# Making the second layer's weight from all partitions, in a fused FFT, soft-MoE and squared-ReLU kernel

## The chip, the core and the metric

The kernel runs on one core of a Trainium2 chip. Its engines are called by the profile's names: PE (matrix multiply; PEld is its weight load), DVE (vector), ACT (activations and copies), POOL (general), SP (issues most DMAs). The metric is the device time of one execution in microseconds, as the median of several runs; less is better.

## The reference

The input x is 8 x 3072 x 256. The reference takes the real part of a two-dimensional FFT, then a soft mixture of experts over tokens, then a feed-forward layer with a squared ReLU:

```python
x = fft(fft(x, axis=1), axis=2).real.reshape(24576, 256)
logits = x @ phi                                # 32 slots, 4 for each of 8 experts
slot_in = softmax(logits, axis=0).T @ x         # 32 x 256
slot_out[e] = relu(slot_in[e] @ w1[e]) @ w2[e]  # w1: 256 x 1024, w2: 1024 x 256
x = softmax(logits, axis=1) @ slot_out
h = x @ w_in                                    # 256 x 2048
out = (s * relu(h)**2 + b) @ w_out              # 2048 x 256
```

## The kernel before, in words

The last two products are turned round: h = c @ G, where c are the 32 softmax coefficients of a token and G = slot_out @ w_in is a 32 x 2048 matrix. Both are held as float16 pairs of a high and a low part, so that a token has 128 numbers, and G (tile g16) has 128 partitions: its high part twice, then its low part twice.

The part that the change touches begins near 199 us of the span. The experts' slots go through w1 (`e_up`, L899) and are turned on PE (`e_turn`, L919). Then `e_down` (L931 to L948) multiplies by w2: experts 0 to 3 are group eg=0, experts 4 to 7 eg=1, and each of a group's four experts sits in its own 32 columns of the PE array (`tile_position=(0, 32 * cg)`). The loop runs over 8 slices f of the hidden features, with the expert cg as the inner loop; half 0 is f = 0 to 3, half 1 is f = 4 to 7. w2 comes through SP's queue (L801 to L814): experts 0 to 3 whole, then the first halves of 4 to 7, then quarters. A float32 product shows as two PE records.

Before `e_down`, the coefficients of chunk 0 are copied on DVE (`c_two`, L779) and turned by two DMA transposes (`c_turn`, L784). After it, PE picks each expert's slots with a selection matrix (L987), ACT copies them out (sot), the largest absolute value is brought to all partitions through two transposes and a product (L1009 to L1023), and one product with four 32-column tiles makes G (L1015). ACT and DVE round it to gs; its first 512 features are copied into g16 by ACT and DVE, the other 1536 by 12 DMAs of 32 partitions each (L1032 to L1034).

The main stage (L1052 to L1142) makes 64 blocks of 384 tokens. For a block, `emit_h(n, p)` makes 256 of the 2048 features of block n: two products into the PSUM tile fhp (pool ps_f, two buffers), ReLU and scale on ACT to r (L1062), max times r on DVE to r2 (L1063). At its end it calls `finish()` (L1039), which takes the previous emission's r2, casts it to float16 (L1048, high part a) and subtracts (L1049, low part l). In block n of `finish`, the cast is ACT's and the subtraction DVE's, but for n < 2 the emissions with p % 4 = 2 have their cast on DVE, and those with p % 4 other than 0 their subtraction on POOL. So the ACT queue holds, in this order, r of an emission and then the cast of the one before it. The order of each queue is the order of the program: the kernel has a manual schedule.

`dots(op, n, t, f)` (L1081) is the work of a unit: one product of 512 columns with the high part and one of 256 columns with the low part, for one of three groups t of 128 tokens and one of 16 feature slices f. A block has 48 units. Blocks 1 to 63 finish one t before the next; between their units the emissions for the following block stand, one for every 6 units. Block 0 goes feature by feature: all three t for each f, so that it can begin once the first emissions are there. Three emissions stand ahead of it, and 13 among its 48 units: its own other five and all eight of block 1. `result` (L1089) scales and adds the bias: on DVE alone in blocks 0 and 63, and by ACT, POOL and DVE in the others.

## Time and profile before

| what | value |
| --- | --- |
| median of 3 runs | 1402.54 us (1401.94 to 1404.03) |
| the profiled execution | 1404.25 us, of which the span is 1402.5 us |
| mean granted TensorE clock | 0.998 |
| DMA, mean over the span | 80 GB/s |

The span is the time from the first to the last instruction of the core. A row of the profile names the line of the kernel, the engine, the operation and its tiles (out<-in); a number behind "idle before" or in brackets is the time the engine stood still just before, with what ended it. The timeline gives the start of a group of like instructions, the time from its first start to its last end, and their count. The windows give, for a stretch, the busy time of each engine and the granted clock.

### The profile page before, as it was taken

What the parts mean: (1) busy time and instruction counts of PE and PEld (TensorE: products, weight loads), DVE (VectorE), ACT (ScalarE), POOL (GpSimd) and SP (SyncE); (2) the same over time, 40 slices, a digit from 0 to 9 for tenths busy, and PEclk for the clock granted to TensorE, in tenths of its full rate; (3) what the DMA queues carried; (4) which work ended last, traced back from release to release, by engine and by line L of the source; (5) the groups of instructions that cost most, each with busy time, mean ns of one, the idle gap of its engine ahead of it and who ended that gap; (6) DMA issues with size and microseconds to landing.
All of it is one profiled execution on the core that took longest, in us unless ns stands there. A gap on an engine that the chain in (4) does not pass through costs nothing.

```text
span 1402.5 us, 23190 instructions
## 1 busy us (share of the span) xinstructions
PE 1379.1 (98%) x9026; PEld 844.8 (60%) x9026; DVE 1151.8 (82%) x1485; ACT 1002.3 (71%) x1407; POOL 316.6 (23%) x290
## 2 busy tenths in 40 slices
PE   9989998999999999999999999999999999999998
PEld 6667554566666666666666666666666666666665
DVE  1567745998989898989898989898888888888885
ACT  2676115787777777778787777777877777777773
POOL 1145202422222121212121212122212121112110
PEclk9999999999999999999999999999999999999999
DMA  8997993101010101011110101010101010101000
GB/s 348 414 318 296 380 410 106 36 24 36 24 33 23 36 21 36 23 32 28 27 30 24 36 24 33 24 36 21 35 23 37 23 37 20 37 23 37 23 20 27
DMA packets 74526, 112.89 MB, mean 80 GB/s; under 512 B 35792, under 2 KB 61264, under 8 KB 67120
## 3 DMA queue, kind: packets, MB, share of 16 engines
q1 hardware_dynamic: 74288, 111.31, 24.0%
q8 instruction: 71, 1.16, 0.4%
q14 instruction: 39, 0.32, 0.1%
q0 software_dynamic: 128, 0.10, 0.0%
HBM read 78.48 MB, written 25.17 MB: 74 GB/s over the span
## 4 chain that ended last, share of the span: by engine, by line
PE 88%; DVE 2%; DMA 1%; ACT 1%; issue 0%; SPq 0%; POOL 0%; ACTq 0%; POOLq 0%; DVEq 0%
PE op L1085 46%; PE op L1087 23%; PE fhp L1058 11%; PE racc L725 3%; DMA w2t<-in_moe_w_dram 1%; PE hp L650 1%; PE dps L710 1%; DVE r L1063 1%; DVE rhl L1049 0%; SPq L1034 0%; PE lp L189 0%; PE lp L567 0%; PE ehp L905 0%; ACT r L1062 0%; DVE cm L582 0%
## 5 line engine op out<-in xcount | busy, mean ns | idle before, releaser
L1085 PE MATMUL op<-whl,rhl 128*128 128x512 f16 x3072 | 1025.9, 379 | 0.0
L1087 PE MATMUL op<-whl,rhl 128*128 128x256 f16 x3072 | 837.4, 273 | 0.3 <-DVE rhl L1049 0.3
L1062 ACT ACTIVATE r<-fhp,wsc 128x768 f32<-128x768 f32 x512 | 458.9, 898 | 157.4 <-PE fhp L1058 154.6
L1063 DVE SCALAR_TENSOR_TENSOR r<-fhp,r 128x768 f32<-128x768 f32 x512 | 484.2, 949 | 25.1 <-ACT r L1062 23.2
L1085 PEld LDWEIGHTS <-rhl 128*128 128x128 f16 x3072 | 300.6, 98 | 335.3
L1049 DVE TENSOR_TENSOR rhl<-r,rhl 128x768 f16<-128x768 f32 x500 | 489.6, 981 | 3.3 <-ACT rhl L1048 0.9
L1048 ACT CAST rhl<-r 128x768 f16<-128x768 f32 x508 | 419.4, 826 | 75.6 <-DVE r L1063 75.3
L1095 POOL TENSOR_TENSOR o<-o,bias 128x256 f32<-128x256 f32 x186 | 203.4, 1094 | 881.2 <-ACT o L1094 876.4
L1087 PEld LDWEIGHTS <-rhl 128*128 128x128 f16 x3072 | 300.6, 98 | 62.5 <-DVE rhl L1049 0.7
L1058 PE MATMUL fhp<-ct,g 128*128 128x384 f16 x1024 | 249.9, 326 | 3.9 <-DVE r L1063 2.9
L1097 DVE SCALAR_TENSOR_TENSOR ot<-op,small,o 128x256 f32<-128x256 f32 x192 | 92.7, 483 | 104.6 <-POOL o L1095 104.3
L1058 PEld LDWEIGHTS <-g 128*128 128x128 f16 x1024 | 100.0, 98 | 71.6 <-issue 4.1
L1094 ACT ACTIVATE o<-op,small 128x256 f32<-128x256 f32 x186 | 88.2, 474 | 17.5 <-PE op L1087 17.4
L393 PE MATMUL vt<-xb,phd 128*64 128x512 f32 (+3 forms) x288 | 47.9, 467 | 5.3 <-DMA xb<-in_x_turned_dram 5.3
L725 PE MATMUL racc<-xrt,dh 128*64 128x256 f32 x384 | 44.5, 383 | 0.4 <-DVE dh L715 0.4
L393 PEld LDWEIGHTS vt<-xb,phd 128*64 128x64 f32 x288 | 25.0, 136 | 26.3 <-issue 8.6
L725 PEld LDWEIGHTS racc<-xrt,dh 128*64 128x64 f32 x384 | 26.3, 137 | 20.9 <-issue 4.9
L418 DVE COPY v<-vq 128x512 f32<-128x512 f32 (+1 forms) x15 | 8.3, 593 | 34.8 <-PE vq L414 34.8
L405 ACT COPY vts<-vt 128x512 f32<-128x512 f32 (+1 forms) x16 | 8.5, 532 | 35.8 <-PE vt L393 35.7
L463 ACT COPY tt<-tps 32x512 f32<-32x512 f32 x48 | 27.7, 576 | 5.3 <-PE tps L449 4.8
L1049 POOL TENSOR_TENSOR rhl<-r,rhl 128x768 f16<-128x768 f32 x12 | 20.1, 1686 | 39.6 <-DMA g<-gs 33.0
L772 POOL TENSOR_TENSOR lg<-lg,rm 112x512 f32<-112x512 f32 x16 | 22.5, 1407 | 4.2 <-DVE rm L770 4.2
...
## 6 DMA issues: line engine op xcount, KB each, us to landing
xb<-in_x_turned_dram SPq DMA_DIRECT2D x24, 1024.0 KB, 20.1
...
out_dram<-ot SPq DMA_DIRECT2D x128, 128.0 KB, 1.7
...
out_dram<-ot SPq DMA_DIRECT2D x128, 64.0 KB, 2.0
...
```

The source lines that it names most:

```text
L393: nc.tensor.matmul(vt[64 * h:64 * h + 64, o:o + k, :], lhsT=phd[:, c, sg, :], rhs=turned(pg, c, i, k, rev), start=(c == 0 and m < 2), stop ...
L725: nc.tensor.matmul(raccs[acc][64 * h:64 * h + 64, :], lhsT=dh[:, m, g].rearrange("p j e -> p (j e)"), rhs=xr[k][0][:, g, t, :], start=(sum ...
L1048: (nc.vector.tensor_copy if n < 2 and p % 4 == 2 else nc.scalar.copy)(a, r2)
L1049: (nc.gpsimd if far else nc.vector).tensor_tensor(out=l, in0=r2, in1=a, op=ALU.subtract)
L1058: nc.tensor.matmul(hp[:, k, :].rearrange("p (s b m) -> p s b m", s=2, b=B), lhsT=g16[:, f * P:(f + 1) * P], rhs=c, start=True, stop=True)
L1062: nc.scalar.activation(out=r, in_=hp, func=AF.Relu, scale=wsc[:, 2, p:p + 1])
L1063: nc.vector.scalar_tensor_tensor(out=r2, in0=hp, scalar=0.0, in1=r, op0=ALU.max, op1=ALU.mult)
L1085: nc.tensor.matmul(op.rearrange("p h d -> p (h d)"), lhsT=a, rhs=w.rearrange("p h d -> p (h d)"), start=(f == 0), stop=False)
L1087: nc.tensor.matmul(op[:, 0, :], lhsT=l, rhs=w[:, 0, :], start=False, stop=(f == NFC - 1))
L1094: nc.scalar.activation(out=o1, in_=op[:, 1, :], func=AF.Copy, scale=qv)
L1095: nc.gpsimd.tensor_tensor(out=o1, in0=o1, in1=bias, op=ALU.add)
L1097: nc.vector.scalar_tensor_tensor(out=ot, in0=op[:, 0, :], scalar=qv, in1=o1, op0=ALU.mult, op1=ALU.add)
```

## The change

* w2: experts 4, 5 and 6 come in two halves each, expert 7 as a half, a quarter and two eighths. In `e_down(1, 1)` the loops are exchanged: the expert cg is the outer loop, the feature slice f the inner.
* Coefficients of chunk 0: no DMA transposes and no copies for them; PE turns them with 32 products (`ct_turn`) between the two groups of `e_down`, and ACT and DVE copy them out.
* Slots: the selection matrix is repeated four times, so that sot has the 32 slots four times in its 128 columns (`e_slots`); the first group's part is done before the second group's `e_down`. The maxima go through a product with the selection matrix (`e_tops`) in place of two transposes and a product.
* G: features 0 to 1023 are made in four products on all 128 rows (`g_dot`), rounded straight into g16 by ACT, and on the low rows by DVE (`g_out`). Features 1024 to 2047 go as before, by 16 DMAs (`g_rest`). Two of the four products, and `g_rest`, stand behind the first two emissions.
* Blocks 0 and 1 both go feature by feature. Two emissions stand ahead of them, and 22 among their 96 units, the first at unit 3 and the last at unit 91, 4.2 units apart on average: the rest of block 0, block 1, and block 2. `finish()` is called ahead of each of these emissions, too. The first unit's products are split in two, so that those with the high part can go first. The sharing of casts and subtractions with DVE and POOL holds for n < 3.
* The warming products (keep_warm) of this part are gone.

The diff, cut to its core:

```diff
-        c = (slice(0, 4), slice(4, 6), slice(0, 8), slice(6, 8))[h]
-        dma_ready(2.57 * (0.5, 0.25, 1, 0.25)[h])
+        c = (slice(0, 4), slice(4, 6), slice(0, 8), slice(4, 8), slice(6, 7), slice(7, 8))[h]
...
-    todo += [(h == 0, lambda e=e, h=h: w2_load(e, h)) for h in (0, 1, 3) for e in range(4, 8)]
+    parts2 = [(e, 0) for e in range(4, 8)] + [(4, 3), (5, 3), (6, 3), (7, 1), (7, 4), (7, 5)]
+    todo += [(h == 0, lambda e=e, h=h: w2_load(e, h)) for e, h in parts2]
...
-    sot = late.tile([P, 2, NE], F32, name="sot")
+    sot = ctp.tile([P, 2, P], F32, name="sot")
...
+    sel4 = ep.tile([P, 2, 4, NE], F32, name="sel4")
+    nc.gpsimd.tensor_copy(sel4, sel_sb.unsqueeze(2).to_broadcast([P, 2, 4, NE]))
+    selm = ep.tile([P, 2, NE], F32, name="selm")
+    id16 = ep.tile([P, P], F16, name="id16")
+    nc.gpsimd.tensor_copy(id16, ident)
...
-        for f in range(4 * half, 4 * half + 4):
-            for cg in range(4):
-                nc.tensor.matmul(
-                    op[32 * cg:32 * cg + 32, :], lhsT=hTs[eg][:, f, 32 * cg:32 * cg + 32],
-                    rhs=w2t[4 * eg + cg][:, f, :],
-                    start=(f == 0), stop=(f == FF1 // P - 1), tile_position=(0, 32 * cg), skip_group_check=True,
-                )
+        fs, cgs = range(4 * half, 4 * half + 4), range(4)
+        for f, cg in [(f, cg) for cg in cgs for f in fs] if eg and half else [(f, cg) for f in fs for cg in cgs]:
...
-        (nc.scalar.copy if eg else nc.vector.tensor_copy)(so[:, eg, :], op)
-        nc.vector.tensor_reduce(out=small[:, 18 + eg:19 + eg], in_=op, axis=AX.X, op=ALU.max, apply_absolute_value=True)
+        if eg:
+            for c in range(2):
+                nc.scalar.copy(so[:, eg, c * P:(c + 1) * P], op[:, c * P:(c + 1) * P])
+        else:
+            nc.vector.tensor_copy(so[:, eg, :], op)
+        top = small[:, 18 + eg:19 + eg]
+        nc.vector.tensor_reduce(out=top, in_=op, axis=AX.X, op=ALU.max, apply_absolute_value=True)
+        nc.vector.tensor_scalar(out=selm[:, eg, :], in0=sel_sb[:, eg, :], scalar1=top, scalar2=None, op0=ALU.mult)
...
+    spt, top4 = [], []
+
+    def e_slots(eg):
+
+        if eg == 0:
+            spt.extend(pse.tile([P, P], F32, tag="sp", name="sp_", bufs=2) for _ in range(2))
+        for c in range(2):
+            nc.tensor.matmul(spt[c], lhsT=so[:, eg, c * P:(c + 1) * P], rhs=sel4[:, eg].rearrange("p r n -> p (r n)"),
+                             start=(eg == 0), stop=(eg == 1))
+
+    def e_tops(eg):
+
+        if eg == 0:
+            top4.append(pse.tile([P, P], F32, tag="tps", name="top4", bufs=1)[:, 0:NE])
+        nc.tensor.matmul(top4[0], lhsT=ones, rhs=selm[:, eg, :], start=(eg == 0), stop=(eg == 1))
...
+        tp = pse.tile([P, 8, P], F16, tag="eh", name="ctt", bufs=3)
+        a = lgc(0).rearrange("p k g e -> p (k g e)").bitcast(F16).rearrange("p (h k m) -> p h k m", h=2, k=8)[:, h]
+        for k in range(8):
+            for q in (0, 64):
+                nc.tensor.transpose(tp[q:q + 64, k, 0:R], a[:, k], id16[:R, :R], tile_position=(0, q))
+        (nc.vector.tensor_copy if h else nc.scalar.copy)(cts[0][:, h], tp[:, :, 0:R])
+
+    e_down(0, 0)
+    e_down(0, 1)
     for h in range(2):
-        c_two(0, h, ep)
-        c_turn(0, h)
-    warm = pse.tile([P, P], F32, tag="mx", name="warm")
-    for eg in range(2):
-        for h in range(2):
-            keep_warm(warm, (0,0,0,0)[2 * eg + h])
-            if eg == 1 and h == 0:
-                while side_step(0.0, True):
-                    pass
-                mxp[:] = [pse, 1]
-                for f in wim_steps[:-1]:
-                    f()
-            e_down(eg, h)
-    for f in wim_steps[-1:]:
+        ct_turn(h)
+    e_slots(0)
+    while side_step(0.0, True):
+        pass
+    mxp[:] = [pse, 1]
+    for f in wim_steps[:-1]:
         f()
+    e_down(1, 0)
+    wim_steps[-1]()
+    nc.vector.tensor_scalar(out=wim, in0=wim, scalar1=D / GMAX, scalar2=None, op0=ALU.mult)
+    e_tops(0)
+    e_down(1, 1)
     drop(hTk[0])
-    keep_warm(warm, 2)
-    sp_ = pse.tile([P, 2, NE], F32, tag="sp", name="sp_")
+    e_slots(1)
+    e_tops(1)
     for c in range(2):
-        for eg in range(2):
-            nc.tensor.matmul(sp_[:, c, :], lhsT=so[:, eg, c * P:(c + 1) * P], rhs=sel_sb[:, eg, :],
-                             start=(eg == 0), stop=(eg == 1))
-    nc.scalar.copy(sot, sp_)
-    keep_warm(warm, 0)
+        nc.scalar.copy(sot[:, c, :], spt[c])
+    qv, ga, gsc = [small[:, k:k + 1] for k in range(15, 18)]
+    nc.vector.tensor_reduce(out=ga, in_=top4[0], axis=AX.X, op=ALU.max)
+    nc.vector.tensor_scalar(out=ga, in0=ga, scalar1=wim, scalar2=1e-15 * D / GMAX, op0=ALU.mult, op1=ALU.max)
+    nc.vector.reciprocal(gsc, ga)
...
-        mt = psf.tile([P, 2, 512], F32, tag="fhp", name="mt")
-        row = small[0:1, 13:14]
-        nc.tensor.transpose(mt[0:1, 0, 0:P], small[:, 18:19], ident)
-        nc.tensor.transpose(mt[0:1, 0, P:2 * P], small[:, 19:20], ident)
-        nc.vector.tensor_reduce(out=row, in_=mt[0:1, 0, 0:2 * P], axis=AX.X, op=ALU.max)
-        gp = pso.tile([P, 512], F32, tag="op", name="gp")
-        for c in range(2):
+        gps = {}
+        HC = 2 * P
+
+        def g_dot(j):
+
+            gps[j] = pso.tile([P, 512], F32, tag="op", name="gp")[:, 0:HC]
+            for c in range(2):
+                nc.tensor.matmul(gps[j], lhsT=sot[:, c, :], rhs=wi[c][:, HC * j:HC * j + HC], start=(c == 0), stop=(c == 1))
+
+        def g_out(j):
+
+            g, gp = g16[:, HC * j:HC * j + HC], gps.pop(j)
+            nc.scalar.activation(out=g, in_=gp, func=AF.Copy, scale=gsc)
+            nc.vector.scalar_tensor_tensor(out=g[64:P], in0=gp[64:P], scalar=gsc[64:P], in1=g[64:P], op0=ALU.mult, op1=ALU.subtract)
+
+        def g_rest():
+
+            gp = pso.tile([P, 512], F32, tag="op", name="gr")[:, 0:HC]
+            for c in range(2):
+                for j in range(4):
+                    nc.tensor.matmul(
+                        gp[32 * j:32 * j + 32, :], lhsT=sot[:, c, 0:NE], rhs=wi[c][:, HC * (4 + j):HC * (5 + j)],
+                        start=(c == 0), stop=(c == 1), tile_position=(0, 32 * j), skip_group_check=True,
+                    )
+            gs = frp.tile([P, 2, HC], F16, tag="r", name="gs")
+            nc.scalar.activation(out=gs[:, 0], in_=gp, func=AF.Copy, scale=gsc)
+            nc.vector.scalar_tensor_tensor(out=gs[:, 1], in0=gp, scalar=gsc, in1=gs[:, 0], op0=ALU.mult, op1=ALU.subtract)
             for j in range(4):
-                nc.tensor.matmul(
-                    gp[32 * j:32 * j + 32, :], lhsT=sot[:, c, :], rhs=wi[c][:, 512 * j:512 * j + 512],
-                    start=(c == 0), stop=(c == 1), tile_position=(0, 32 * j), skip_group_check=True,
-                )
-            if c == 0:
-                nc.tensor.matmul(mt[:, 1, 0:1], lhsT=ones[0:1, :], rhs=row, start=True, stop=True)
-                nc.vector.tensor_scalar(out=ga, in0=mt[:, 1, 0:1], scalar1=wim, scalar2=1e-15 * D / GMAX,
-                                        op0=ALU.mult, op1=ALU.max)
-                nc.vector.reciprocal(gsc, ga)
-        warm = pso.tile([P, 512], F32, tag="op", name="warm")[:, 0:P]
-        keep_warm(warm, 6)
-        gs = frp.tile([P, 2, 512], F16, tag="r", name="gs")
-        nc.scalar.activation(out=gs[:, 0], in_=gp, func=AF.Copy, scale=gsc)
-        nc.vector.scalar_tensor_tensor(out=gs[:, 1], in0=gp, scalar=gsc, in1=gs[:, 0], op0=ALU.mult, op1=ALU.subtract)
-        for r in range(4):
-            eng = nc.vector.tensor_copy if r // 2 else nc.scalar.copy
-            eng(g16[32 * r:32 * r + 32, 0:512], gs[0:32, r // 2])
-        for j in range(1, 4):
-            for r in range(4):
-                nc.sync.dma_start(out=g16[32 * r:32 * r + 32, 512 * j:512 * j + 512], in_=gs[32 * j:32 * j + 32, r // 2])
+                for r in range(4):
+                    nc.sync.dma_start(out=g16[32 * r:32 * r + 32, HC * (4 + j):HC * (5 + j)], in_=gs[32 * j:32 * j + 32, r // 2])
+
+        for j in range(2):
+            g_dot(j)
+        for j in range(2):
+            g_out(j)
...
-                far = n < 2 and p % 4
-                (nc.vector.tensor_copy if n < 2 and p % 4 == 2 else nc.scalar.copy)(a, r2)
+                far = n < 3 and p % 4
+                (nc.vector.tensor_copy if n < 3 and p % 4 == 2 else nc.scalar.copy)(a, r2)
...
-        def dots(op, n, t, f):
+        def dots(op, n, t, f, part=2):
...
-            nc.tensor.matmul(op.rearrange("p h d -> p (h d)"), lhsT=a, rhs=w.rearrange("p h d -> p (h d)"),
-                             start=(f == 0), stop=False)
-            nc.tensor.matmul(op[:, 0, :], lhsT=l, rhs=w[:, 0, :], start=False, stop=(f == NFC - 1))
+            if part != 1:
+                nc.tensor.matmul(op.rearrange("p h d -> p (h d)"), lhsT=a, rhs=w.rearrange("p h d -> p (h d)"),
+                                 start=(f == 0), stop=False)
+            if part:
+                nc.tensor.matmul(op[:, 0, :], lhsT=l, rhs=w[:, 0, :], start=False, stop=(f == NFC - 1))
...
-        for p in range(3):
+        for p in range(2):
             emit_h(0, p)
-            keep_warm(warm, (0,4,0)[p])
-        ops = [pso.tile([P, 2, D], F32, tag="op", name="op") for _ in range(3)]
-        units = [(f, t) for f in range(NFC - 2) for t in range(3)]
+        g_dot(2)
+        g_out(2)
+        g_rest()
+        g_dot(3)
+        g_out(3)
+        finish()
+        units = [(f, t) for t in range(3) for f in range(2)] + [(f, t) for f in range(2, NFC - 2) for t in range(3)]
         units += [(f, t) for t in range(3) for f in (NFC - 2, NFC - 1)]
-        at = [k * 48 // (16 - 3) for k in range(16 - 3)]
-        for u, (f, t) in enumerate(units):
-            while at and at[0] <= u:
-                at.pop(0)
-                emit_h(*divmod(16 - len(at) - 1, 8))
-            dots(ops[t], 0, t, f)
-            if u == 27:
-                nc.vector.tensor_tensor(out=qv, in0=ga, in1=ga, op=ALU.mult)
-                nc.vector.tensor_tensor(out=qv, in0=qv, in1=wa, op=ALU.mult)
-                nc.vector.tensor_tensor(out=qv, in0=qv, in1=sb_in[:, 0:1], op=ALU.mult)
-                for k in wik:
-                    drop(k)
-            if f == NFC - 1:
-                result(ops[t], 0, t)
-        for k in rhk.pop(0):
-            drop(k)
-        for n in range(1, NBLK):
+        first = [(0, t) for t in range(3)] + [(1, t) for t in range(3)] + units[6:]
+        emits = {3 + k * 21 // 5: divmod(k + 2, 8) for k in range(22)}
+        for n, order in enumerate((first, units)):
+            ops = {}
+            for u, (f, t) in enumerate(order):
+                if 48 * n + u in emits:
+                    finish()
+                    emit_h(*emits.pop(48 * n + u))
+                if f == 0:
+                    ops[t] = pso.tile([P, 2, D], F32, tag="op", name="op")
+                if n == 0 and f == 0:
+                    dots(ops[t], n, t, f, 0)
+                else:
+                    dots(ops[t], n, t, f)
+                if n == 0 and (f, t) == (0, 2):
+                    for k in range(3):
+                        dots(ops[k], n, k, f, 1)
+                if n == 0 and u == 27:
+                    nc.vector.tensor_tensor(out=qv, in0=ga, in1=ga, op=ALU.mult)
+                    nc.vector.tensor_tensor(out=qv, in0=qv, in1=wa, op=ALU.mult)
+                    nc.vector.tensor_tensor(out=qv, in0=qv, in1=sb_in[:, 0:1], op=ALU.mult)
+                    for k in wik:
+                        drop(k)
+                if n and u in (8, 20):
+                    c_two(1, u // 20, frp)
+                if n and u in (14, 26):
+                    c_turn(1, u // 26)
+                if f == NFC - 1:
+                    result(ops[t], n, t)
...
+        for n in range(2, NBLK):
```

## Rows read from the trace of the kernel before

**Rows 1.** The page's first part: busy time, share of the span, instructions.

```profile
PE 1379.1 (98%) x9026; PEld 844.8 (60%) x9026; DVE 1151.8 (82%) x1485; ACT 1002.3 (71%) x1407; POOL 316.6 (23%) x290
```

**Rows 2.** Windows of blocks 0, 1 and 2: length, busy us, clock, DMA share, GB/s.

```profile
231.39:253.75 22.36, 20.63 (x122) 11.54 (x120) 19.60 (x24) 18.64 (x24) 16.23 (x10) 1.00 0.03 9
253.75:272.78 19.03, 18.52 (x112) 10.94 (x112) 17.41 (x26) 13.95 (x18) 5.89 (x5) 1.00 0.24 58
272.78:290.98 18.20, 18.20 (x114) 10.96 (x112) 16.86 (x23) 14.50 (x21) 6.96 (x6) 1.00 0.06 20
```

**Rows 3.** Waits of PE, 225 to 265 us: total, times, longest.

```profile
PE fhp L1058 <- DVE r L1063: 2.9, 7, 0.8
```

**Rows 4.** Timeline, PE and DVE, 183 to 213 us.

```profile
183.23 1.02 PE L710 MATMUL dps<-ht__1653,ft_sb 128*128 128x512 f32 x2
184.19 3.67 PE L725 MATMUL racc<-xrt,dh 128*64 128x256 f32 x32
...
209.14 4.35 PE L937 MATMUL eop<-w2t,hT 128*32 128x256 f32 x70
...
212.87 0.42 DVE L944 COPY so<-eop 128x256 f32<-128x256 f32 x1 [1.91 <-PE eop L937]
```

**Rows 5.** The tile of w2: durations in ns (least, median, most), first and last start.

```profile
L937 PE MATMUL eop<-w2t,hT x128: 379/379/403, 209.1 to 220.3; 128*32 128x256 f32 x128
```

**Rows 6.** Timeline of PE's weight loads, the last wait for w2.

```profile
219.59 0.57 PEld L937 LDWEIGHTS eop<-w2t,hT 128*32 128x32 f32 x10 [0.58 <-DMA w2t<-in_moe_w_dram]
```

**Rows 7.** Timeline from w2's end to the first emission, 220 to 228 us.

```profile
220.68 0.37 ACT L944 COPY so<-eop 128x256 f32<-128x256 f32 x1 [12.84 <-PE eop L937]
...
221.08 0.42 DVE L945 TENSOR_REDUCE small<-eop 128x1 f32<-128x256 f32 x1 [7.45 <-ACT so L944]
...
226.21 7.92 SPq L1034 DMA_DIRECT2D g<-gs  x12
...
227.74 0.81 PE L1058 MATMUL fhp<-ct,g 128*128 128x384 f16 x4 [0.82 <-DVE g L1031]
```

**Rows 8.** Timeline of ACT and DVE at the first emissions, 228 to 231 us.

```profile
228.26 1.69 ACT L1062 ACTIVATE r<-fhp,wsc 128x768 f32<-128x768 f32 x2 [0.80 <-PE fhp L1058]
...
229.19 1.82 DVE L1063 SCALAR_TENSOR_TENSOR r<-fhp,r 128x768 f32<-128x768 f32 x2 [1.60 <-ACT r L1062]
...
230.18 0.83 ACT L1048 CAST rhl<-r 128x768 f16<-128x768 f32 x1 [0.23 <-DVE r L1063]
...
230.92 0.89 ACT L1062 ACTIVATE r<-fhp,wsc 128x768 f32<-128x768 f32 x1
```

**Rows 9.** Timeline of DVE, PE and ACT, 248 to 260 us.

```profile
248.13 0.55 DVE L1048 CAST rhl<-r 128x768 f16<-128x768 f32 x1
248.60 0.95 DVE L1063 SCALAR_TENSOR_TENSOR r<-fhp,r 128x768 f32<-128x768 f32 x1
...
256.02 0.49 PE L1058 MATMUL fhp<-ct,g 128*128 128x384 f16 x2
...
258.66 0.83 ACT L1048 CAST rhl<-r 128x768 f16<-128x768 f32 x1 [2.32 <-DVE r L1063]
259.40 1.69 ACT L1062 ACTIVATE r<-fhp,wsc 128x768 f32<-128x768 f32 x2
```

**Rows 10.** The page's costliest groups: busy us, mean ns, idle before.

```profile
L1095 POOL TENSOR_TENSOR o<-o,bias 128x256 f32<-128x256 f32 x186 | 203.4, 1094 | 881.2 <-ACT o L1094 876.4
...
L1097 DVE SCALAR_TENSOR_TENSOR ot<-op,small,o 128x256 f32<-128x256 f32 x192 | 92.7, 483 | 104.6 <-POOL o L1095 104.3
...
L1094 ACT ACTIVATE o<-op,small 128x256 f32<-128x256 f32 x186 | 88.2, 474 | 17.5 <-PE op L1087 17.4
...
L1049 POOL TENSOR_TENSOR rhl<-r,rhl 128x768 f16<-128x768 f32 x12 | 20.1, 1686 | 39.6 <-DMA g<-gs 33.0
```

**Rows 11.** Windows, as rows 2, of two stretches with little PE work.

```profile
104.00:108.00 4.00, 2.26 (x24) 1.68 (x18) 3.97 (x8) 1.19 (x4) 0.00 (x0) 0.75 1.00 416
228.00:232.00 4.00, 2.62 (x17) 1.60 (x14) 2.77 (x4) 3.51 (x5) 0.00 (x0) 1.00 0.20 53
```

More of the change, by code (lines that the diff above doesn't have):

```diff
@@ L611, in tile_fft2__then__softmoe__then__act_relu2 @@
     tpool.release()
-    late = tc.alloc_tile_pool(name="late", bufs=1)
     hpool = tc.alloc_tile_pool(name="hpool", bufs=1)
@@ new lines, in ct_turn @@
+    def ct_turn(h):
+        if h == 0:
+            cts[0] = ctp.tile([P, 2, B, R], F16, name="ct", bufs=1)
+        tp = pse.tile([P, 8, P], F16, tag="eh", name="ctt", bufs=3)
[4 more added lines that the diff above has]
+        (nc.vector.tensor_copy if h else nc.scalar.copy)(cts[0][:, h], tp[:, :, 0:R])
@@ L991, in tile_fft2__then__softmoe__then__act_relu2 @@
+    nc.vector.reciprocal(gsc, ga)
     pse.release()
     ep.release()
-    qv, ga, gsc = [small[:, k:k + 1] for k in range(15, 18)]
-    nc.vector.tensor_scalar(out=wim, in0=wim, scalar1=D / GMAX, scalar2=None, op0=ALU.mult)
     for _ in range(2):
@@ new lines, in tile_fft2__then__softmoe__then__act_relu2 @@
+        for n, order in enumerate((first, units)):
[25 more added lines that the diff above has]
+                    result(ops[t], n, t)
+            for k in rhk.pop(n):
+                drop(k)
@@ L1143, in tile_fft2__then__softmoe__then__act_relu2 @@
     ctp.release()
-    late.release()
     pools[1][0].release()
```

6 lines of the change are left out of this document (added).

## The prediction

> **What bounds the kernel now.** Read the totals first: PE is busy for 98% of the span [rows 1], so only PE's work and its gaps count. The windows then say where the gaps are. Block 2 is dense: 18.20 us for 48 units and 8 emissions [rows 2]. A unit streams 512 + 256 columns and an emission 2 x 384, so each takes 18.20/56 = 0.325 us. From the first unit at 231.39 us to the start of block 2 at 272.78 us 41.4 us pass [rows 2], and 96 units and the 20 emissions in between need 116 x 0.325 = 37.7 us. So blocks 0 and 1 hold 3.7 us of gaps, and PE's waits name what ends most of them: the DVE's r2 (L1063), which frees the buffer that an emission writes [rows 3]. All after 272.78 us is the same work before and after the change. What the change can give or cost is therefore read from one number: how long after w2's last product block 2 starts. That product starts at 220.3 us [rows 5], so now it is 52.5 us. I call its start E now and E' after.
>
> **Part a, E' itself: +3.0 us.** Now the last wait for w2 ends at 219.59 us [rows 6]: the transfers set E. Afterwards PE has more to do ahead. The first 64 records of w2 begin at 209.14 us, and the last starts 0.38 us before the copy at 212.87 us, so at 212.5 us: 0.053 us a record [rows 4, 5]. Behind them come 32 small products that turn the coefficients. No row shows them; bounds are half of that step, 0.9 us, and the 0.106 us of a record in 64 columns ((3.67 - 0.38)/31 [rows 4]), 3.4 us. I take the narrow tiles' 0.053, 1.7 us: they are the nearest. Then four passes of 128 columns for the slots, each half of the 0.213 us worked out below: 0.4. The first half of the second group takes 32 x 0.053 = 1.7, and w_in's maximum, its copy and the product for the first tops, one behind the other, 0.9: no row has them at these sizes; they lie between nothing and three steps of 0.38 us [rows 5, 7]. That is 217.2 us.
>
> Now the exchanged loop. Two float32 passes of 512 columns end 1.02 us after the first start [rows 4]: twice the streaming of 512 columns and one drain. One pass of 256 columns lasts 0.38 us [rows 5]: its streaming and one drain. The difference is three times the streaming of 256 columns, which is 0.213 us. The 0.106 us in 64-column tiles and the 0.053 us in 32-column tiles are that number divided by two and by four: neighbouring records run side by side because they lie in different tiles. With the expert outside, eight records in a row lie in one tile, and nothing runs beside them. An expert then holds PE for 7 x 0.213 + 0.05 us until the next begins: 3 x 1.54 + 1.49 = 6.1 us in all, where 32 x 0.053 = 1.7 would do. E' = 223.3, which is +3.0. Bounds: if the passes overlapped after all, the transfers would set the end, now with two records in place of ten behind the last piece, -0.7; with slow turns +3.9. The smaller pieces of expert 7 therefore gain nothing: PE comes to them late. The removed DMA transposes lay behind w2 in SP's queue, and I cost that at nothing.
>
> **Part b, from E' to the first emission: -3.5 us.** Now 227.74 - 220.3 = 7.4 us [rows 5, 7]. After: 0.38 for the product; two half copies on ACT, between 0.37 (one whole) and 0.74, taken 0.5; the DVE's maximum 0.42, which again follows ACT's copy [rows 7]; the product with the selection about 0.2 on DVE (between 0 and 0.48, a DVE operation on 256 columns [rows 10]); the two passes for the tops 0.4. Four 256-column passes for G go beside three small DVE operations and end at 2.9 us; ACT's rounding takes 0.47 and DVE's 0.48 [rows 10]: 3.9 us. The added copies on POOL (the repeated selection, the float16 identity) lie ahead of the turns, beside `e_up` and w2's first group, where POOL has no work; without that cover they would cost some 1.1 us each, as a POOL operation on 256 columns does [rows 10].
>
> **Part c, the emissions: the step that decides.** `finish()` is now called ahead of each emission among the units, so ACT's queue holds the cast of the previous emission in front of the next r. The cast waits for r2, r2 for r. Rows of the first emissions give this chain: r starts at 228.26, r2 ends at 230.14, the cast starts at 230.18, and the next instruction of ACT at 230.92 [rows 8]. So from one r to the next 2.66 us must pass, where the program gives 4.2 units and an emission, 1.69 us. Block 1 has one such place already (the `finish()` at unit 5): the products for the next r were issued at 256.02, but ACT stood at the cast until 258.66 and took up r at 259.40 [rows 9].
>
> One emission in four has its cast on DVE. There the next r is not held (0.85 us a piece [rows 8]); its r2 starts behind r2 and cast on DVE, 1.92 + 0.47 us after the r before [rows 8, 9], ends 0.95 later, and with 0.03 and 0.74 the r after that stands 4.11 us behind. Four emissions take 2.66 + 2.66 + 4.11 = 9.4 us, 2.36 each. PE cannot run ahead of it, since fhp has two buffers: an emission waits for the r2 of the one two before it.
>
> The first emission among the units needs G's third part. Second emission at E' + 4.8; cast of the first 4.4 + 1.92 to 7.15; DVE's subtraction to 8.2; rounding on DVE 0.48: E' + 8.6. From there to block 2's first emission are 22 steps, 22 x 2.36 = 51.9: E' + 60.5, against 52.5 now. Parts b and c together: +8.0 us. The first half of G in the pause, the split first units and the 16 small transfers (0.66 us each, 7.92/12 [rows 7], about 10.6 us from E' + 8) lie under this chain. Bounds +6.5 (head 0.8 shorter, first gaps shared) to +10 (DVE subtractions slowed beside POOL).
>
> **Part d, block 2: +1.5 us.** Block 1 now ends for all three t within its last five units. Three bias additions of 1.09 us on POOL, behind subtractions of 1.69 us for block 2, hold DVE's last step of each result, and so the next r2 [rows 10]. Between 0, if the gaps of part c leave POOL ahead, and 3. I take the middle.
>
> **Sum.** +3.0 + 8.0 + 1.5 = +12.5 us on the profiled execution (span 1402.5, its own time 1404.25, 1.7 above the median). The median becomes 1402.54 + 12.5 = 1415.0 us. About 0.2%, 2.8 us, can be told from no change.
>
> **Rivals.** First, *faster*: the cast ahead of r costs nothing because something holds PE's emissions further apart than the chain needs, or ACT reaches the cast with r2 done. It decides at a distance of 2.36 us between emissions. Then 118 pieces of 0.325 us follow the first unit at E' + 7.7: block 2 at E' + 46.1, -6.4 us, with part a -3.4: 1399.1 us. The gaps of rows 3 speak against it; for it only that the program places them 1.69 us apart. Chance 0.10.
>
> Second, *no change*: the same, but today's 3.7 us of gaps stay: +0.3, 1402.8 us. Chance 0.06.
>
> Third, *the clock*: with 28% gaps PE falls to half clock, 1.2 GHz. In a stretch with PE busy for 2.26 of 4 us the mean granted clock was 0.75, so half of it at the lower level; with 2.62 of 4 us it stayed at 1.00 [rows 11]. An emission's share of 1.69 us would take 3.38, 22 x (3.38 - 2.36) = 22 us more: 1437 us. The Trainium skill (TensorE: Matmul & The Clock Gate, section "A second HAM failure mode: psum-queue depth-cycling") says that frequent short idling between groups of matmuls can make the clock swing between its levels. The second of rows 11, the nearer to the forecast's 72%, speaks against it. Chance 0.03.
>
> That the exchanged loop does what it is for (last piece, two records) is the lower bound of part a: 1411.3, inside the forecast.
>
> **How the numbers follow.** The forecast has 0.81: its bounds are -0.7 + 6.5 + 0 = +5.8 and +3.9 + 10 + 3 = +16.9, so 1408 to 1420, and I give 1407 to 1420. Outside lie the three rivals with 0.19. Faster 0.10, same 0.06, slower 0.84.
>
> **What will show it.** ACT's casts (L1048) preceded by waits for r2, some 16 times; PE's waits for L1063 near 15 us in blocks 0 and 1; emissions 2.4 us apart; w2's last product near 223 us with no wait for w2 before it; first emission some 4 us later. If emissions come 1.7 us apart, part c is wrong and with it the sign.

## The result and the profile after

The changed kernel takes 1415.72 us (median of 5 runs, 1414.81 to 1416.79) against 1402.54 us: a ratio of 1.0091, 95% interval 1.0076 to 1.0105. It is slower by 13.2 us. Its profiled execution took 1415.72 us with a span of 1414.0 us.

First the page of the changed kernel: busy time and share, then two groups of instructions (busy us, mean ns, idle before and what ended it).

```profile
PE 1380.4 (98%) x9050; PEld 846.4 (60%) x9050; DVE 1148.7 (81%) x1484; ACT 1002.0 (71%) x1410; POOL 325.2 (23%) x298
...
L1090 ACT CAST rhl<-r 128x768 f16<-128x768 f32 x506 | 417.6, 825 | 92.5 <-DVE r L1105 92.4
...
L1100 PE MATMUL fhp<-ct,g 128*128 128x384 f16 x1024 | 250.1, 326 | 12.0 <-DVE r L1105 11.2
```

PE does 1.3 us more work than before [rows 1]. Most of the rest is waiting: 11.2 us of it ahead of the emissions, for DVE's r2 (2.9 us before [rows 3]). The line numbers have moved: r is now L1104, r2 L1105, the cast L1090, the emission's products L1100.

To compare stretches I count from the experts' first upward product, which is untouched: 198.85 us before, 196.03 us after. The front part before it differs by 2.8 us between the two profiled executions although nothing in it was changed: over the profiled executions of this document this product starts between 193.85 us (e8) and 200.03 us (e10). The timeline of PE from there:

```profile
207.43 3.64 PE L942 MATMUL eop<-w2t,hT 128*32 128x256 f32 x58 [0.47 <-DMA w2t<-in_moe_w_dram]
211.00 0.98 PE L1001 MATMUL ctt<-id,lg 112*64 112x112 f16 x32
...
212.55 1.93 PE L942 MATMUL eop<-w2t,hT 128*32 128x256 f32 x32
...
215.38 4.59 PE L942 MATMUL eop<-w2t,hT 128*32 128x256 f32 x32
...
222.02 1.97 PE L1049 MATMUL gp<-wi,sot 128*128 128x256 f32 x8 [0.38 <-DVE small L1025]
224.26 0.50 PE L1100 MATMUL fhp<-ct,g 128*128 128x384 f16 x2 [0.28 <-DVE g L1055]
```

The exchanged loop is the one of 4.59 us, the loop with the feature outside the one of 1.93 us above it. Three cuts through the records of the exchanged loop (the tile of w2 with durations in ns, then first and last start) show how it runs:

```profile
L942 PE MATMUL eop<-w2t,hT x4: 379/379/403, 215.4 to 216.1; 128*32 128x256 f32 x4
...
L942 PE MATMUL eop<-w2t,hT x6: 379/379/379, 217.4 to 217.8; 128*32 128x256 f32 x6
...
L942 PE MATMUL eop<-w2t,hT x4: 379/379/379, 219.0 to 219.6; 128*32 128x256 f32 x4
```

The first four and the last four records start 0.216 us apart (0.24 us the first time); the 24 between come in pairs, one pair for every 0.216 us. Four records, one for each expert, last 0.40 us in place of 0.38 us and wait for a piece of w2; they start at 215.38, 216.28, 217.17 and 218.06 us. I read this so: the records of one expert, which lie in one tile, do not overlap, but PE takes up the next expert beside the fifth of the eight records of the one before. An expert then holds the next back by 0.89 us, and the mean over the loop is (4.59 - 0.38)/31 = 0.136 us a record, against (1.93 - 0.38)/31 = 0.050 us with the feature outside.

The last record starts at 219.60 us, 23.56 us after the first upward product (21.41 before, where it starts at 220.26 us). The first emission follows 4.67 us later (7.48 before).

The windows of blocks 0, 1 and 2 (length, busy time of PE, PEld, DVE, ACT, POOL, clock, DMA share, GB/s), to be set against [rows 2]:

```profile
228.34:254.29 25.95, 20.81 (x121) 11.54 (x120) 17.19 (x23) 14.55 (x20) 12.49 (x8) 1.00 0.04 11
254.29:282.20 27.91, 20.43 (x118) 11.14 (x116) 16.99 (x25) 17.14 (x23) 13.79 (x9) 1.00 0.13 31
282.20:302.44 20.24, 18.52 (x113) 10.94 (x113) 16.58 (x24) 14.84 (x23) 11.63 (x10) 1.00 0.10 30
```

Blocks 0 and 1 hold 5.1 and 7.5 us of gaps (length less PE's busy time; 1.7 and 0.5 before). PE is busy for 80% and 73% of them, and no other engine for more than 66%: none is full. Block 2 begins 86.17 us after the first upward product (73.93 before) and block 3 106.41 us after it (92.13 before): 14.3 us more. A block begins here with the first emission that stands among its units (it makes features of the next block). What fills the gaps is a chain between engines. Waits of PE, 212 to 300 us:

```profile
PE fhp L1100 <- DVE r L1105: 11.2, 14, 1.5
PE op L1128 <- DVE ot L1141: 1.8, 1, 1.8
```

And the timeline of ACT in block 1:

```profile
256.77 0.83 ACT L1090 CAST rhl<-r 128x768 f16<-128x768 f32 x1 [1.02 <-DVE r L1105]
257.50 0.90 ACT L1104 ACTIVATE r<-fhp,wsc 128x768 f32<-128x768 f32 x1
260.32 0.83 ACT L1090 CAST rhl<-r 128x768 f16<-128x768 f32 x1 [1.92 <-DVE r L1105]
261.06 1.69 ACT L1104 ACTIVATE r<-fhp,wsc 128x768 f32<-128x768 f32 x2
```

ACT stands idle at a cast that waits for r2, and the next r, whose input is there, comes right behind the cast. That is the chain of part c.

### The profile page after: what moved, and what is told of

It is laid out like the page before. It is cut to its first block, busy times and chain, and to the rows that moved or that the text cites. A ratio compares the mean times of both kernels' runs of the same rounds, so it can differ in the third digit from the quotient of the medians.

```text
span 1414.0 us, 23249 instructions
## 1 busy us (share of the span) xinstructions
PE 1380.4 (98%) x9050; PEld 846.4 (60%) x9050; DVE 1148.7 (81%) x1484; ACT 1002.0 (71%) x1410; POOL 325.2 (23%) x298
## 4 chain that ended last, share of the span: by engine, by line
PE 88%; DMA 7%; DVE 3%; ACT 1%; issue 0%; POOL 0%; ACTq 0%; DVEq 0%; POOLq 0%
PE op L1128 45%; PE op L1131 23%; PE fhp L1100 12%; PE racc L724 3%; DMA raw<-in_moe_w_out_dram 1%; DMA xb<-in_x_turned_dram 1%; DMA w2t<-in_moe_w_dram 1%; DVE r L1105 1%; DMA xrt<-in_x_pages_dram 1%; DMA htab_t<-in_htab_dram 1%; PE vt L393 1%; PE hp L649 1%; PE dps L709 1%; PE eop L942 1%; ACT r L1104 1%; PE warm L189 1%
## 5 line engine op out<-in xcount | busy, mean ns | idle before, releaser
L1104 ACT ACTIVATE r<-fhp,wsc 128x768 f32<-128x768 f32 x512 | 458.4, 898 | 154.7 <-PE fhp L1100 153.6
L1105 DVE SCALAR_TENSOR_TENSOR r<-fhp,r 128x768 f32<-128x768 f32 x512 | 483.9, 948 | 37.5 <-ACT r L1104 35.5
L1091 DVE TENSOR_TENSOR rhl<-r,rhl 128x768 f16<-128x768 f32 x494 | 480.7, 975 | 6.8 <-ACT rhl L1090 4.5
L1090 ACT CAST rhl<-r 128x768 f16<-128x768 f32 x506 | 417.6, 825 | 92.5 <-DVE r L1105 92.4
L1100 PE MATMUL fhp<-ct,g 128*128 128x384 f16 x1024 | 250.1, 326 | 12.0 <-DVE r L1105 11.2
L1100 PEld LDWEIGHTS <-g 128*128 128x128 f16 x1024 | 99.9, 98 | 81.1 <-issue 13.6
L393 PE MATMUL vt<-xb,phd 128*64 128x384 f32 (+3 forms) x288 | 47.4, 467 | 2.0 <-DMA xb<-in_x_turned_dram 2.0
L1091 POOL TENSOR_TENSOR rhl<-r,rhl 128x768 f16<-128x768 f32 x18 | 29.6, 1643 | 53.7 <-ACT rhl L1090 47.5
L771 POOL TENSOR_TENSOR lg<-lg,rm 112x512 f32<-112x512 f32 x16 | 22.5, 1406 | 4.2 <-DVE rm L769 4.2
```

Of the source, the lines that this page charges most:

```text
L393: nc.tensor.matmul(vt[64 * h:64 * h + 64, o:o + k, :], lhsT=phd[:, c, sg, :], rhs=turned(pg, c, i, k, rev), start=(c == 0 and m < 2), stop ...
L1090: (nc.vector.tensor_copy if n < 3 and p % 4 == 2 else nc.scalar.copy)(a, r2)
L1091: (nc.gpsimd if far else nc.vector).tensor_tensor(out=l, in0=r2, in1=a, op=ALU.subtract)
L1100: nc.tensor.matmul(hp[:, k, :].rearrange("p (s b m) -> p s b m", s=2, b=B), lhsT=g16[:, f * P:(f + 1) * P], rhs=c, start=True, stop=True)
L1104: nc.scalar.activation(out=r, in_=hp, func=AF.Relu, scale=wsc[:, 2, p:p + 1])
L1105: nc.vector.scalar_tensor_tensor(out=r2, in0=hp, scalar=0.0, in1=r, op0=ALU.max, op1=ALU.mult)
```

## The experiments

Each kernel ran beside the kernel before on the same chip; the ratio is to that. The kernel before had medians of 1403.94 to 1404.76 us beside e1 to e12, so rows of different runs are compared by the ratio and not by the median. The two columns of stretches come from the profiled execution, in us from the experts' first upward product to the first emission among the units of block 2 and of block 3. The expectations say ScalarE, VectorE and GpSimd for ACT, DVE and POOL; a step is the time from the start of one emission to that of the next, and the parts of (n, p) are what emission p of block n leaves.

| kernel | to block 2 | to block 3 | median us | ratio, 95% interval |
|---|---|---|---|---|
| before | 73.93 | 92.13 | 1402.54 | |
| changed | 86.17 | 106.41 | 1415.72 | 1.0091 (1.0076 to 1.0105) |
| e1 finish behind | 81.12 | 101.81 | 1412.95 | 1.0061 (1.0038 to 1.0085) |
| e2 feature outside | 84.19 | 104.42 | 1414.52 | 1.0073 (1.0048 to 1.0099) |
| e3 before + finish ahead | 83.14 | 101.35 | 1412.35 | 1.0064 (1.0041 to 1.0086) |
| e4 = e1 + e2 | 77.16 | 97.84 | 1411.15 | 1.0046 (1.0027 to 1.0064) |
| e5 new head, old blocks | 76.06 | 94.26 | 1405.77 | 1.0013 (0.9984 to 1.0041) |
| e6 = e4, small ones moved | 75.12 | 96.30 | 1406.33 | 1.0016 (1.0007 to 1.0025) |
| e7 changed, casts on DVE | 84.26 | 105.80 | 1415.24 | 1.0079 (1.0065 to 1.0094) |
| e8 = e5, small ones moved | 75.15 | 93.37 | 1403.36 | 0.9991 (0.9971 to 1.0012) |
| e9 = e6 mended | 73.20 | 92.93 | 1403.67 | 0.9986 (0.9966 to 1.0006) |
| e10 changed, results on DVE | 85.08 | 104.42 | 1417.75 | 1.0080 (1.0048 to 1.0112) |
| e11 = e9 + finish ahead | 83.14 | 102.96 | 1414.45 | 1.0062 (1.0039 to 1.0085) |
| e12 = e9, block 1 by token | 78.56 | 97.16 | 1407.60 | 1.0019 (0.9995 to 1.0042) |

### e3: the order alone, put into the kernel before

```diff
             while at and at[0] <= u:
                 at.pop(0)
+                finish()
                 emit_h(*divmod(16 - len(at) - 1, 8))
```

> The kernel before with one thing of the change alone: finish() ahead of each of the 13 emissions among block 0's units. Theory: 13 steps of 2.36 us (30.7 us) in place of the 22.7 us that they take now: 8 us more, 1410.5 us. Rival (an earlier cast is harmless or helps, the slowness of the changed kernel comes from the order of blocks 0 and 1): within 1 us of 1402.5 us.

Measured: 1412.35 us, block 3 9.2 us later than before. Waits of PE and, below, the timeline of ACT in e3 (r2 is L1063 and the cast L1048, as before):

```profile
PE fhp L1058 <- DVE r L1063: 11.4, 15, 1.3
```

```profile
236.19 0.90 ACT L1062 ACTIVATE r<-fhp,wsc 128x768 f32<-128x768 f32 x1
238.11 0.83 ACT L1048 CAST rhl<-r 128x768 f16<-128x768 f32 x1 [1.02 <-DVE r L1063]
238.85 0.90 ACT L1062 ACTIVATE r<-fhp,wsc 128x768 f32<-128x768 f32 x1
240.84 0.83 ACT L1048 CAST rhl<-r 128x768 f16<-128x768 f32 x1 [1.09 <-DVE r L1063]
241.58 1.69 ACT L1062 ACTIVATE r<-fhp,wsc 128x768 f32<-128x768 f32 x2
```

The wait of [rows 3] grows from 2.9 to 11.4 us by one line, and r follows r after 2.66 and 2.73 us. The order by itself makes the pace.

### e1, e2 and e4: the order and the loop taken back

```diff
                 if 48 * n + u in emits:
-                    finish()
                     emit_h(*emits.pop(48 * n + u))
```

> The changed kernel without the finish() ahead of the emissions among the units, so that ACT's queue has r before the cast of the emission before it, as in the kernel before. Theory (the cast ahead of r sets the pace, 2.36 us an emission): the 22 steps fall from 52.0 us to 22 x 1.69 = 37.2 us plus gaps like the 3.7 us of the kernel before, so 10 to 11 us less than the changed kernel, 1405 us; PE's waits for r2 fall from 11.2 us to about 3. Rival (the gaps come from POOL's subtractions or the results, and the order of the queue only shows them): at most 1.5 us less, 1414 us or more.

```diff
-        for f, cg in [(f, cg) for cg in cgs for f in fs] if eg and half else [(f, cg) for f in fs for cg in cgs]:
+        for f, cg in [(f, cg) for f in fs for cg in cgs]:
```

> The changed kernel with the loops of the last half of w2 as before: feature slice outside, expert inside. Theory (records that follow each other in one tile of 32 columns don't overlap): the 32 records take 32 x 0.053 = 1.7 us in place of 4.2 us, and all behind them moves up by 2.5 us: 1413.2 us. Rival (the transfers of w2 set the end in both orders): PE waits for expert 7's last eighth, and the gain is under 0.5 us: 1415.2 us or more.

> The changed kernel with both undone: r before the cast, and the feature slice outside in w2's last half. Theory (the two costs are on one path and add): 10.5 + 2.5 = 13 us less than the changed kernel, 1402.7 us, as fast as the kernel before. Rival (the shorter way to the first emission now shows in full, and blocks 0 and 1 are as dense as before): 2.8 us faster than the kernel before, 1399.7 us.

Measured: e1 1412.95 us, e2 1414.52, e4 1411.15. e2's last w2 record comes 2.0 us sooner than the changed kernel's, but 1.1 us of that is a wait for the first pieces of w2 (the 0.47 us at 207.43 and the weight loads behind it), which e2 does not have. Against e1, with the exchanged loop and without that wait, e4 gains 1.0 us (22.48 and 21.48 us after the first upward product). So the loop is worth 1.0 us and not 2.5, and with the feature outside PE waits for w2 again, as the rival has it (0.38 us in e2).

e1 gains 4.6 us to block 3 where 10 were expected, and falls between the theory and its rival; e4 stays 5.7 us behind the kernel before. The 4.6 us are not the price of the order alone: 1.1 us of them is the wait for w2, which e1 does not have, and e1 lost 3.0 us against e4 from the first unit to block 2, where its clock fell twice (shown with e6). e2 and e4 differ by this order alone and have a granted clock of 1.00 throughout these blocks: 104.42 against 97.84 us, so 6.6 us. In e1 most steps are now 1.6 to 2.1 us, but three are 3.8 to 4.0, and 3.3, 2.9 and 2.4 us stand where the clock is lower. Waits of PE in e1:

```profile
PE fhp L1100 <- DVE r L1105: 6.5, 4, 2.2
PE op L1131 <- POOL rhl L1091: 1.3, 1, 1.3
```

Four waits now make 6.5 us. So a second theory was needed: behind the chain stand other stalls, which the slow pace had hidden. Two of the long waits follow VectorE instructions that take long beside GpSimd. They can be seen in the changed kernel too; its timeline of DVE at qv (the factor of the results, three one-column products):

```profile
243.68 0.96 DVE L1172 TENSOR_TENSOR small<-small 128x1 f32<-128x1 f32 x1
244.68 0.16 DVE L1173 TENSOR_TENSOR small<-small 128x1 f32<-128x1 f32 x1
244.87 1.50 DVE L1174 TENSOR_TENSOR small<-small,sb_in 128x1 f32<-128x1 f32 x1
```

and of POOL at the same time:

```profile
242.98 3.37 POOL L1091 TENSOR_TENSOR rhl<-r,rhl 128x768 f16<-128x768 f32 x2 [0.74 <-DVE rhl L1090]
```

One column takes 0.16 us where DVE is let through and up to 1.50 us where it is not; the last one ends with POOL's second subtraction, at 246.4 us. The Trainium skill (SBUF — State Buffer, section "Who interferes with whom") says that a VectorE instruction with two SBUF inputs contends with a GpSimd instruction that reads SBUF, that the port pair the two share is an exclusive lock, and that the order of issue decides who blocks. These rows agree: POOL's two subtractions lie at 242.98 and 244.71 us, 1.64 us each; DVE's first product ends with the first of them, its short one stands in the pause between, and its last ends with the second.

### e6: the small instructions moved

```diff
     nc.vector.reciprocal(gsc, ga)
+    nc.vector.tensor_tensor(out=qv, in0=ga, in1=ga, op=ALU.mult)
+    nc.vector.tensor_tensor(out=qv, in0=qv, in1=wa, op=ALU.mult)
+    nc.vector.tensor_tensor(out=qv, in0=qv, in1=sb_in[:, 0:1], op=ALU.mult)
...
-                if n and u in (8, 20):
-                    c_two(1, u // 20, frp)
-                if n and u in (14, 26):
-                    c_turn(1, u // 26)
...
-                if n % 4 == 1 and n // 4 + 1 < NCH:
+                if (n == 2 or n % 4 == 1) and n // 4 + 1 < NCH:
```

The same three lines leave unit 27 of block 0.

> e4 with the three one-column products for qv put right behind the reciprocal, where VectorE waits anyway, and the two copies of coefficients put from block 1 to block 2. Theory (two of e4's four long gaps come from VectorE instructions that wait for GpSimd's subtraction): the two gaps of 2.1 and 2.2 us go, start of block 3 at 93.5 us after the first upward product (97.8 in e4), 1407 us. Rival (any slip puts the parts out of step, and another gap takes the place): at 97 us or later, 1411 us.

Measured: 1406.33 us, as the theory said, but block 3 at 96.3 us, nearer to the rival's 97 than to the theory's 93.5. Both long steps are gone (3.9 and 4.0 us in e4, 1.62 and 1.62 in e6). To block 3 it is only 1.5 us less than e4, because of three things: 0.9 us of the head (a w2 piece came later), 0.5 us in block 2, where the two copies now stand (21.2 us in place of 20.7), and a new pair of steps, 3.0 and 2.3 us, behind the gap at the parts of (0,2). Windows of e6 around it:

```profile
234.00:236.00 2.00, 1.50 (x9) 0.67 (x7) 1.48 (x3) 1.22 (x3) 0.24 (x1) 1.00 0.10 25
236.00:238.00 2.00, 0.67 (x5) 0.40 (x5) 0.90 (x1) 0.63 (x1) 2.00 (x2) 1.00 0.10 25
238.00:242.00 4.00, 4.00 (x16) 1.87 (x15) 1.82 (x2) 1.62 (x2) 1.00 (x1) 0.57 0.07 16
```

From 234 to 238 us PE was busy for 2.17 us; then the granted clock is 0.57, mostly at the lower level, 1.2 GHz. e1 shows it too, 0.83 in two stretches of 10 us behind its long gaps (250 to 260 and 270 to 280 us). But a gap like this is not always followed by a fall. The same place of e4, and a place of e12 with still less work, kept 1.00, there and behind:

```profile
232.00:236.00 4.00, 2.16 (x13) 0.99 (x11) 1.77 (x3) 1.65 (x3) 3.10 (x2) 1.00 0.11 26
...
259.00:263.00 4.00, 1.69 (x11) 0.58 (x9) 1.69 (x2) 1.62 (x2) 3.22 (x2) 1.00 0.00 0
```

What decides it stays open. e4's profiled execution had no fall in these blocks and took 1407.30 us, below its median of 1411.15.

### e9, and e11 with one line more

```diff
-                far = n < 3 and p % 4
+                far = n < 3 and p % 4 and (n, p) != (0, 2)
...
-            if n in (0, NBLK - 1):
+            if n in (0, 1, NBLK - 1):
...
-        emits = {3 + k * 21 // 5: divmod(k + 2, 8) for k in range(22)}
+        emits = {2 + k * 21 // 5: divmod(k + 2, 8) for k in range(22)}
...
+                    if pend and pend[0][1] % 4 == 2:
+                        finish()
                     emit_h(*emits.pop(48 * n + u))
```

> e6 with three more edits: the low part of (0,2) on VectorE, its emission one unit earlier and its finish ahead of the next emission (as for every part whose cast is on VectorE, so that ScalarE's queue keeps r first); block 1's results on VectorE, without GpSimd's addition. Theory (e6's rest is two places: the gap of 2.6 us at (0,2)'s parts with the half clock behind it, 3.9 us in all, and VectorE's 2.5 us wait for GpSimd at block 2's start, 2 us): start of block 3 at 90 us after the first upward product (96.3 in e6, 92.1 before), block 2 in 18.7 us, 1402 us or less. Rival (any gap closed opens another further on, since the emissions run at the rate of the engines behind them): 94 us or more, 1405 us or more.

e11 has the same with the condition left out, so that every finish is ahead of its emission again:

> e9 with finish ahead of every emission again, nothing else. Theory (the queue's order by itself gives the pace of 2.36 us, whatever else is mended): the steps fall back from e9's mean of 1.9 to 2.36 us, start of block 2 at 81 us after the first upward product (73.2 in e9, 86.2 in the changed kernel), start of block 3 at 100.5 or later (92.9 in e9), 1411 us. Rival (the order is worth only what putting finish behind gave in the changed kernel, 4.6 us, and the rest is what e6 and e9 mended): start of block 2 at 78 us or before, 1408 us or less.

Measured: e9 1403.67 us, block 3 at 92.9 us, between the theory's 90 and the rival's 94; e11 1414.45 us, block 3 at 103.0. Waits of PE, 220 to 300 us, in e9 and then in e11:

```profile
PE fhp L1103 <- DVE r L1108: 2.3, 6, 0.8
```

```profile
PE fhp L1103 <- DVE r L1108: 10.5, 16, 1.2
```

Waits of ACT, 226 to 272 us, again e9 and then e11:

```profile
ACT r L1107 <- PE fhp L1103: 8.0, 10, 1.3
ACT rhl L1093 <- DVE r L1108: 2.8, 5, 1.1
```

```profile
ACT rhl L1093 <- DVE r L1108: 16.2, 13, 1.9
ACT r L1107 <- PE fhp L1103: 1.5, 3, 0.9
```

In e9 ACT waits at r for PE, so it is ahead of PE. In e11 it waits at the cast for DVE and PE waits for it. One condition costs 10.0 us to block 3, near e3's 9.2; the rival, that the order is worth only e1's 4.6 us, falls.

### e7: the casts taken out of ACT's queue

```diff
-                (nc.vector.tensor_copy if n < 3 and p % 4 == 2 else nc.scalar.copy)(a, r2)
+                (nc.vector.tensor_copy if n < 3 else nc.scalar.copy)(a, r2)
```

> The changed kernel with every cast of the first three blocks on VectorE, finish still ahead of the emission. Theory (the pace is set by the cast standing ahead of r in ScalarE's queue): without the cast in that queue the steps fall from 2.36 us to what VectorE and the program allow, 1.9 to 2.0 us (0.96 + 0.56 a step, 0.96 more in one of four), start of block 2 at 78 us after the first upward product (86.2 in the changed kernel), 1407 us. Rival (the emission's pace is not the queue's order but what comes behind it, the subtractions on GpSimd and their lateness): as little as putting finish behind gave, 81 us or more, 1411 us or more.

Measured: 1415.24 us, block 2 at 84.3. By its numbers the rival came true, but the run doesn't show its reason: the edit put another limit in place. Timeline of DVE in e7:

```profile
247.42 1.23 DVE L1090 CAST rhl<-r 128x768 f16<-128x768 f32 x1
248.69 0.96 DVE L1091 TENSOR_TENSOR rhl<-r,rhl 128x768 f16<-128x768 f32 x1
249.56 0.95 DVE L1105 SCALAR_TENSOR_TENSOR r<-fhp,r 128x768 f32<-128x768 f32 x1
250.55 0.56 DVE L1090 CAST rhl<-r 128x768 f16<-128x768 f32 x1
251.02 0.95 DVE L1105 SCALAR_TENSOR_TENSOR r<-fhp,r 128x768 f32<-128x768 f32 x1
252.01 1.24 DVE L1090 CAST rhl<-r 128x768 f16<-128x768 f32 x1
```

DVE has no gap here, and both casts that meet a POOL subtraction (at 246.60 and 251.19 us) take 1.2 us in place of 0.56. My estimate had no room for that.

### e5 and e8: the new head with the old blocks

```diff
-        finish()
+        emit_h(0, 2)
+        ops = [pso.tile([P, 2, D], F32, tag="op", name="op") for _ in range(3)]
...
```

Then come the loops of before, from units on, with its `n < 2` in finish; the feature is outside in the experts. e8 adds e6's move of the three products.

> The changed head (w2's last expert in eighths, coefficients turned on PE, first half of G made on all rows) with the feature outside, in front of the old blocks: three emissions ahead, 13 in block 0, casts behind r, block 1 token by token. Theory (the head alone gains, the two loops are what lose): the last w2 record as before (21.5 us after the first upward product), the first emission 4.7 us behind it instead of 7.4, the first unit about 9 us behind it instead of 11.1, blocks 0 and 1 then 22.4 and 19.0 as before: start of block 3 at 90.0 us after the first upward product (92.1 before), 1400.4 us. Rival (the gain stops at the second half of G, whose 16 transfers now leave later and are wanted 3 units after the first): PE waits 1.5 us or more for g, start of block 3 at 92 or later, 1402.5 us or more.

> e5 with the three one-column products for qv behind the reciprocal. Theory: in block 0 they stand beside GpSimd's subtraction and cost up to 1.5 us on VectorE; with them away block 0 is 0.5 to 1 us shorter than e5's: 1399.7 us, the fastest so far. Rival: the block's emissions hide them, and the time is e5's within 0.2 us.

Measured: 1405.77 and 1403.36 us. Waits of PE in e5:

```profile
PE fhp L1100 <- DVE r L1105: 2.4, 5, 0.8
PE fhp L1100 <- DMA g<-gs: 2.2, 3, 1.0
PE fhp L1100 <- DVE g L1055: 1.8, 4, 0.7
```

The rival holds: the first emission comes 4.7 us behind w2 as expected, but the first unit 10.95 us (11.13 before), since the second half of G now stands between the emissions, and its transfers are waited for 2.2 us. The head gains nothing by itself: e5 reaches block 3 2.1 us later than the kernel before. e8 is 0.9 us shorter than e5 to block 3, as expected, but not the fastest. Neither e5, e8 nor e9 can be told from the kernel before.

### e10 and e12: block 2's start

e10 is the changed kernel with e9's second edit alone. e12 is e9 with

```diff
-        for n, order in enumerate((first, units)):
+        for n, order in enumerate((first, [(f, t) for t in range(3) for f in range(NFC)])):
```

> The changed kernel with block 1's three results on VectorE (as block 0's) in place of ScalarE and GpSimd, nothing else. Theory (block 2's 2 us are VectorE's wait for GpSimd's additions, which stand behind a subtraction in GpSimd's queue): block 2 from its first emission to block 3's falls from 20.24 us to 18.5, 1413.9 us. Rival (block 2 waits for the three results because they end together, whoever makes them): 20 us, 1415.5 us.

> e9 with block 1 token by token (its last part is emitted 8 units into it), so that its three results are 5 us apart. Theory (the 1.5 us that e9's block 2 still has over 18.2 are the three results together): block 2 in 18.7 us, start of block 3 at 91.9 us after the first upward product, 1402.7 us. Rival (token by token wants all parts of block 1 in its first 16 units, and the last of them are late): a gap of 1 us or more in block 1, start of block 3 at 93 us or later, 1404 us.

Measured: in e10 block 2 takes 19.34 us (20.24 in the changed kernel, 18.5 expected). Half of what was lost is POOL's, the other half is that three results stand together, for DVE now spends 2.8 us on them ahead of an r2. The medians can't tell: 1417.75 us, and the two intervals overlap. In e12 block 2 takes 18.60 us, as the theory said, but block 1 wants its parts too early, as the rival said; waits of PE in e12:

```profile
PE op L1134 <- POOL rhl L1094: 3.2, 3, 1.3
```

Two steps of 3.0 and 4.7 us follow, and 1407.60 us in all. Of the 4.2 us that it comes later to block 3 than e9, 1.5 us lie in the head, where w2 came later.

## Why the prediction was right, and where its terms were off

The forecast was 1415.0 us, measured 1415.72. The sum of +12.5 us stands against 14.3 us on the path of the profiled executions (2.2, 10.1 and 2.0 us by parts) and 13.2 us in the medians. The sign and the mechanism, the pace of part c, were right. That the median is met to 0.7 us is luck: part a came out 0.8 us too large and the start of part c 2.0 us too early, and the two errors pull against each other.

**Part a, +3.0, was too large.** The prediction's step of 0.213 us inside one tile held (0.216), but not its "nothing runs beside them": an expert holds the next back by 0.89 us and not 1.54, so the loop took 4.2 us from its first to its last start in place of 6.1. The 32 turns took 0.98 us, not 1.7. The profiled executions show +2.2, but 1.1 of it is the wait for the first w2 pieces. Of the kernels with the same loop e7 has that wait too (last record 23.7 us after the first upward product); e1 and e10 do not (22.5, so +1.1). The direction was right: without that wait PE sets the end and not the transfers, and e4, whose records wait for w2 again, ends 1.0 us sooner than e1. The upper bound of part a does not follow from its own terms: slow turns add 1.7 us, so +4.7 and not +3.9, which moves the end of the range by 0.8 us and changes nothing else.

**Part b, -3.5, measured -2.8.** PE waits 0.38 us for DVE's reading of the maximum ahead of the products of G, which the estimate had beside them. The rest of the 0.7 us was not taken apart.

**Part c was the step that decided, and it held.** From the first unit's emission to block 2's first are 22 steps in 51.97 us, 2.36 each; the prediction has 22 x 2.36 = 51.9. The pattern 2.66, 2.66 and 4.11 us for two is there further on (2.72, 2.66, then 1.62 and 2.50). But the total agrees to 0.1 us by luck: the first five steps are 1.6 to 2.3 us, while two further on are 3.3 (qv beside POOL) and 3.75 (a result not yet read, the 1.8 us of PE's second wait), which the prediction did not have. The start was 10.6 us behind w2 and not 8.6, as the emission stands behind the first units and these behind G's second half; so b and c together are +10.1, against +8.0, and just past the upper bound of +10.

That it is the order of ACT's queue was shown in both directions: put into the kernel before it costs 9.2 us (e3), put into e9 10.0 us (e11). Taking it out of the changed kernel gave back only 4.6 us (e1), or 6.6 us where neither the wait for w2 nor the clock disturbs the comparison (e4 against e2). That the pace alone explained the loss, as e1's expectation had it, was wrong: the small VectorE instructions (e6), the late parts of (0,2) and the results over GpSimd (e9) stand behind it.

**Part d, +1.5, measured +2.0**, with the cause as named in half: e10 and e12 give the other half to the results' standing together.

**The rivals.** Among the kernels with the new blocks, long rows of emissions 1.6 us apart come only where finish is behind (e1, e4, e6, e9 and e12); so *faster* fell by its own point of decision, 2.36 us, and *no change* with it. *The clock* did not fall in the changed kernel's blocks (1.00 in all three windows), but it did in e1 and e6, behind long gaps. There it cost about 1.7 us each time (an estimate: 17% of 10 us in e1), not 22 in all.

**The signs.** ACT's casts were preceded by 16 waits for r2, as forecast, and the emissions were 2.36 us apart. PE's waits for r2 were 11.2 us and not 15. The first pieces of w2 were waited for, the last ones not.

## What to carry to other kernels

An instruction that waits in ACT's queue held all that was queued behind it (e3, e11): put the start of the new tile ahead of the finish of the old one, and count the whole cycle through the engines (here 2.66 us against 1.69 us of PE work). When such a step is taken out, expect the stalls that it had hidden, and try the one line in both kernels before giving it a price. A shorter way to the first instruction of a stage was worth nothing here (e5), as the work removed from there stood in front of the third.

## What the chip showed beside this

Records in one 32-column tile step by 0.216 us, and over four tiles in turn four of them come in that time: 4 times. The Trainium skill (TensorEngine Tiling (Array Packing), section "Theoretical Speedup") has up to 4 times for four tiles; the rows here agree. Where eight records in a row lie in one tile, PE still begins the next tile beside the fifth, so that the exchanged loop took 2.7 times the other's step (0.136 and 0.050 us) and not 4.

A VectorE cast of 128x768 with a single SBUF input also waits for GpSimd: 0.56 us alone, 1.23 us in e7 beside a subtraction. The second operation from PSUM (L1105), with one SBUF input, keeps its 0.95 us.

In e6 the clock was 0.57 behind 4 us with 1.8 us of gaps, while e4 kept 1.00 behind the same gaps, e12 with 2.3 us of gaps in 4, and blocks 0 and 1 of the changed kernel with gaps of 5.1 and 7.5 us spread over 26 and 28 us.
